# Decode attention over a key and value cache beside a small MLP: TensorE's program as loops, values always in one slot, part of w4 behind the last values

## The chip, the cores and the metric

The kernel runs on one core of a Trainium2 chip. The time is the device time of one execution in microseconds (us), the median of several. A profile of one execution is at hand beside it; its span runs from the first to the last instruction of the core.

## The reference

One token `x` (1024 values) goes through two branches and their sum is added to it.

```python
xn = _layernorm(x)
return x + _A_ref(xn, K, V, wq, wo) + _B_ref(xn, w1, w2, w3, w4)

# A: 32 query heads, 4 key/value heads, 65536 keys of 128 values each
q = (xn @ wq)                                # 1024 x 4096
p = softmax(q k^T * 128 ** -0.5)             # eight query heads share one K, V
A = (p @ v) @ wo                             # 4096 x 1024
# B: one position, so the shifted h is zero
hs = shift(gelu(layernorm(xn) @ w1)) @ w2    # 1024 x 1024 each
x1 = xn + hs
B = x1 + gelu(layernorm(x1) @ w3) @ w4       # 1024 x 3584, 3584 x 1024
```

All inputs are bf16. K and V are 67.1 MB each, the weights some 35.7 MB: 169.87 MB that are read once.

## The kernel before

**Slots and loads.** SBUF holds three slots of 32768 bf16 columns (8.39 MB over 128 partitions). K and V are cut into eight tiles (g, r): four heads g, two halves r of 32768 keys. `items` (L193 to L201) is the order of loads: wq, K(0,0), V(0,0), w3, K(0,1), V(0,1), wa (w1 and the first 14 rows of w4), then K and V in turn, wb (w4's last 14 rows and w2) ahead of the last V, and wo in five pieces. Item i goes to slot i mod 3 (L208), wo to the slot of the last K. All loads are issued by SyncE in program order (`load`, L211); each waits (L229) until what was computed from the slot's last content is done. The main loop (L566) computes item i and then issues the load of item i + 3.

**Order of work.** `Flow` is a small hand-written scheduler: it counts per engine, and each instruction waits on the counts of those that wrote or read its operands (L41). Engines run in the order of the program text.

**Products of one row.** q, w1's and w3's products (`rows_product`, L314 to L326) run unrolled, four column groups of TensorE at once. Weight rows of w2, w4 and wo (`rows_loop`, L328 to L341) run in TensorE loops (`Fori`): two or five rows per pass, two matmuls of 512 columns for each row, all adding up in `psR`. The last 22 rows of wo (`row_acc`, L534) run in four column groups.

**A K tile** (`compute_K`, L442): VectorE transposes the slot in four quarters `cg` (L449); after two quarters (after each, in the last tile) TensorE runs a loop of four passes over them, four or eight matmuls of 512 columns against `qst` (L455), into the four banks `sc`. Then the row maxima (L462), two small transposes on TensorE (L463, L468), the exponential on ScalarE (L471), and a transpose of the weights on VectorE (L473).

**A V tile** (`compute_V`, L495): 64 matmuls (L503) into `oacc`. The first half of a head is copied to `ob` (L509); after the second, `group_end` (L513) weights and adds both halves on VectorE, normalizes, and writes the columns `oT` that wo's rows are multiplied with.

**The end.** After the last `group_end` come wo's rows; the first ten rows' sum is folded into the output banks (L548, L549, L558), the last rows follow, and 2 KB go out (L561).

Of the kernel before, what the change touches and what calls it, by code (L numbers as in the profile page):

```python
# [16 lines left out]
WO_PIECES = (10, 10, 8, 3, 1)  # L17
WO_UNROLL = 5
CGS = 2


class Flow:


    def __init__(self, nc, ctx):
        self.nc = nc
        self.ctx = ctx
        self.engines = {"T": nc.tensor, "V": nc.vector, "S": nc.scalar, "G": nc.gpsimd, "Q": nc.sync}
        self.sems = {}
        self.counts = {}  # L30
        self.seen = {e: {} for e in self.engines}
        self.writer = {}
        self.readers = {}

    def sem(self, name):
        if name not in self.sems:
            self.sems[name] = self.ctx.enter_context(self.nc.semaphore(f"s_{name}"))
            self.counts[name] = 0
        return self.sems[name]

    def _wait(self, eng, reads, writes):  # L41
# [7 lines left out]
        for key in reads:  # L49
            if key in self.writer:  # L50
                token = self.writer[key]
                if token[0] != "T" or eng != "T":
                    add(token)
        for key in writes:
            if key in self.writer:
                token = self.writer[key]
                if token[0] != "T" or eng != "T":
                    add(token)
            for token in self.readers.get(key, ()):
                if token[0] != eng:  # L60
                    add(token)
        for name, value in need.items():
            if self.seen[eng].get(name, 0) < value:
                self.engines[eng].wait_ge(self.sem(name), value)
                self.seen[eng][name] = value
# [8 lines left out]
    def op(self, eng, reads, writes, emit, times=1):  # L74

        self._wait(eng, reads, writes)
        sem = self.sem(eng)

        def signal(ins):
            ins.then_inc(sem, 1)  # L80

        emit(signal)
        self.counts[eng] += times
        self._note((eng, self.counts[eng]), reads, writes)
# [8 lines left out]
    def one(self, eng, reads, writes, call):  # L93
        self.op(eng, reads, writes, lambda signal: signal(call(self.engines[eng])))
# [3 lines left out]
def kernel(  # L98
# [28 lines left out]
    assert S == 1 and DH == P and REP == 8 and HQ == 32 and DC == 8 and NOUT == 1024  # L127
# [4 lines left out]
    FW = F // 8  # L132
    assert FW <= 512 and F % 8 == 0 and FW % 16 == 0 and FW // 16 == FC and OC == 32
    NQ = NOUT // 4
    NH = NOUT // 2
    FH = FC // 2
# [9 lines left out]
    slots = [tile_sb([P, KEYS], BF16, f"slot{i}") for i in range(SLOTS)]  # L146
    work = tile_sb([P, HF * 512], BF16, "work")
    ob = tile_sb([P, 512], F32, "ob")
    xpad = tile_sb([P, DC, 32], BF16, "xpad")
    QS = P + 24  # L150
    qst = [tile_sb([P, 4, QS], BF16, f"qst{i}") for i in range(2)]
    qsel = tile_sb([P, 4, HQ], BF16, "qsel")
    ident_bf = tile_sb([P, P], BF16, "ident_bf")
    ident_f = tile_sb([P, P], F32, "ident_f")
    og = tile_sb([P, P + 1], F32, "og")
    msk = tile_sb([P, 4, 32], F32, "msk")
    hstrip = tile_sb([P, 192], BF16, "hstrip")
    gsel = tile_sb([P, P], BF16, "gsel")
    sel32 = tile_sb([P, 32], F32, "sel32")
    sel8 = tile_sb([P, 8], F32, "sel8")  # L160
    sel8x = tile_sb([P, 32], F32, "sel8x")
    mask16 = tile_sb([P, 16], F32, "mask16")
    mask64 = tile_sb([P, 64], F32, "mask64")
# [3 lines left out]
    lnb = tile_sb([P, 8, DC], F32, "lnb")  # L167
    x_bf = tile_sb([P, DC], BF16, "x_bf")
    xn2b = tile_sb([P, DC], BF16, "xn2b")
    qT = tile_sb([P, HQ], BF16, "qT")  # L170
    hf_f = tile_sb([P, FC], F32, "hf_f")
    hT = tile_sb([P, FC], BF16, "hT")
    gT = tile_sb([P, DC], BF16, "gT")
    o5 = tile_sb([P, 32], F32, "o5")
    oT = tile_sb([P, OC], BF16, "oT")
    rep = msk[0:1].rearrange("p a b -> p (a b)")

    sc = ps.tile([P, HF, 512], F32, name="sc")
    oacc = ps.tile([P, 512], F32, name="oacc")
    pm = ps.tile([P, 512], F32, name="pm")  # L180
    psR = ps.tile([P, 2, 512], F32, name="psR")
    psB = sc[:, 0, :]
# [7 lines left out]
    assert sum(WO_PIECES) == OC  # L190
    wo_start = [sum(WO_PIECES[:i]) for i in range(len(WO_PIECES))]

    items = [("wq",), ("K", 0, 0), ("V", 0, 0), ("w3",)]  # L193
    for g in range(HKV):
        for r in range(NT):
            if (g, r) != (0, 0):
                items += [("K", g, r), ("V", g, r)]
            if (g, r) == (0, 1):
                items += [("wa",)]
    items.insert(len(items) - 1, ("wb",))  # L200
    items += [("wo",)]  # L201
# [4 lines left out]
    one, op = fl.one, fl.op  # L206

    slot_of = [i % SLOTS for i in range(len(items))]  # L208
    slot_of[-1] = slot_of[items.index(("K", HKV - 1, NT - 1))]

    def load(i):  # L211
        item, s = items[i], slot_of[i]
        t, kind = slots[s], items[i][0]
# [4 lines left out]
        elif kind == "wa":  # L218
            loads = [(0, w1_v), (KEYS // 2, w4_v[:, 0:FH * NOUT])]
        elif kind == "wb":  # L220
            loads = [(0, w4_v[:, FH * NOUT:FC * NOUT]), (KEYS // 2, w2_v)]
# [3 lines left out]
        else:  # L225
            cache = A_k_cache if kind == "K" else A_v_cache
            _, g, r = item
            loads = [(0, cache[0, g, r * KEYS:(r + 1) * KEYS, :].rearrange("(p k) d -> p (k d)", p=P))]
        fl._wait("Q", [], [("slot", s), ("slot", s, 1)] + [("slot", s, q) for q in range(2, 5)] + [("kt", s, cg) for cg in range(4)])  # L229
        for n, (at, src) in enumerate(loads):  # L230
            key = ("slot", s) if n == 0 else ("slot", s, n)
            fl.dma("Q", f"slot{s}" if n == 0 else f"slot{s}_{n}", [], [key], t[:, at:at + src.shape[-1]], src)

    qrow = work[:, 0:1024].rearrange("p (b n) -> p b n", b=2)
    psel = work[:, 1024:1536].rearrange("p (b m) -> p b m", b=4)
    ones_f = og[:, 0:P]
    xr = work[:, 1536:2048]

    load(0)
    fl.dma("S", "x", [], ["x_bf"], x_bf[:], A_x[0, 0, :].rearrange("(p c) -> p c", c=DC))  # L240
    load(1)
    load(2)
    one("G", [], ["xr"], lambda e: e.memset(xr[0:33, :], 0.0))
    fl.dma("S", "x2", [], ["xr"], xr[0:33:32, :], A_x[0, 0, :].rearrange("(j n) -> j n", j=2))

    def ident(t, key):
        one("G", [], [key], lambda e: e.memset(t[:], 0.0))
        one("G", [key], [key], lambda e: e.affine_select(
            out=t[:], in_=t[:], compare_op=ALU.not_equal, fill=1.0, base=0, pattern=[[-1, P]],
            channel_multiplier=1))  # L250

    eps_t, negmean, rstd, ln_s1, ln_s2 = (sm[:, i:i + 1] for i in range(5))
    ident(ident_bf, "ident_bf")
    ident(ident_f, "ident_f")
    one("G", [], ["eps"], lambda e: e.memset(eps_t, LN_EPS))
    one("G", [], ["ones"], lambda e: e.memset(ones_f, 1.0))
    one("G", [], ["xpad"], lambda e: e.memset(xpad[:], 0.0))
    one("G", [], [("qst", 0)], lambda e: e.memset(qst[0][:], 0.0))
    one("G", [], [("qst", 1)], lambda e: e.memset(qst[1][:], 0.0))
    one("G", [], ["hstrip"], lambda e: e.memset(hstrip[:], 0.0))  # L260

    def v(reads, writes, call):
        one("V", reads, writes, call)

    v(["ident_f"], ["sel32"], lambda e: e.tensor_tensor(out=sel32[:], in0=ident_f[:, 0:32], in1=ident_f[:, 32:64], op=ALU.add))
    v(["ident_f", "sel32"], ["sel32"], lambda e: e.tensor_tensor(out=sel32[:], in0=sel32[:], in1=ident_f[:, 64:96], op=ALU.add))
    v(["ident_f", "sel32"], ["sel32"], lambda e: e.tensor_tensor(out=sel32[:], in0=sel32[:], in1=ident_f[:, 96:128], op=ALU.add))
    v(["sel32"], ["mask16"], lambda e: e.tensor_tensor(out=mask16[:], in0=sel32[:, 0:16], in1=sel32[:, 16:32], op=ALU.add))
    v(["ident_f"], ["mask64"], lambda e: e.tensor_tensor(out=mask64[:], in0=ident_f[:, 0:64], in1=ident_f[:, 64:128], op=ALU.add))
    v(["sel32"], ["dmask"], lambda e: e.reduce_sum(out=dmask[:], in_=sel32[:].rearrange("p (cg h) -> p cg h", h=8), axis=AX.X))  # L270
    v(["sel32"], ["mask4"], lambda e: e.reduce_sum(out=mask4[:], in_=sel32[:].rearrange("p (x dd) -> p dd x", dd=4), axis=AX.X))
    v(["sel32"], ["sel8"], lambda e: e.reduce_sum(out=sel8[:], in_=sel32[:].rearrange("p (cg h) -> p h cg", h=8), axis=AX.X))
    v(["sel8"], ["sel8x"], lambda e: e.tensor_copy(out=sel8x[:].rearrange("p (h dd) -> p h dd", dd=4),
                                                   in_=sel8[:].unsqueeze(2).to_broadcast([P, 8, 4])))
    iv = ident_bf[:].rearrange("p (b i r) -> p b r i", b=2, r=2)
    for b in range(2):
        for par in range(2):
            v(["ident_bf"], [("psel", b, par)], lambda e: e.tensor_copy(
                out=psel[:, 2 * b + par, :].rearrange("p (a i) -> p a i", a=4),
                in_=iv[:, b, par, :].unsqueeze(1).to_broadcast([P, 4, 32])))  # L280
    psel_keys = [("psel", b, par) for b in range(2) for par in range(2)]
    lead = ident_bf[:].rearrange("p (j u) -> p j u", u=32)[:, :, 0]
    v(["ident_bf", "hstrip"], ["hstrip"], lambda e: e.tensor_copy(
# [322 lines left out]
```

## Time and profile before

| | |
|---|---|
| median of 3 runs | 402.4 us (402.27 to 402.55) |
| the profiled execution | 402.23 us |
| its span | 400.1 us |
| TensorE, matmuls | 223.5 us busy, 1407 |
| VectorE | 210.5 us busy |
| ScalarE, GpSimd | 30.9 and 6.3 us busy |
| read from memory | 169.87 MB, 425 GB/s over the span |
| granted TensorE clock, mean | 0.803 |

The page has the busy time of each engine, the span in 40 slices of 10 us with a digit for the busy share in tenths, the load queues, and the chain of work that ended last, followed back from the last instruction. The chain in order of time is a view of its own: start, duration, what. "issue" in it is time for which no wait is seen. A row of the view of waits says which engine waited at which line for whom, the total, how often, and the longest.

### The profile page before, as it was taken

The numbers are of one execution on the slowest core, as the hardware profiler recorded it, in microseconds if no ns is written. First come the engines' busy times: TensorE is split into PE (matmuls) and PEld (weight loads), VectorE is DVE, ScalarE is ACT, GpSimd is POOL, SyncE is SP. The second block draws the span as 40 slices with busy tenths as digits, with TensorE's granted clock in tenths as the row PEclk, the third lists the DMA queues.
The fourth block names the chain that finished last, engine by engine and source line by source line (L and its number), as shares of the span: only waits on it lengthen the run. The fifth ranks groups of instructions, "written<-read, shape, count | busy, mean of one in ns | idle before, by whom it ended". The sixth has DMA issues, their size and how long they took to land.

```text
span 400.1 us, 4118 instructions
## 1 busy us (share of the span) xinstructions
PE 223.5 (56%) x1407; PEld 91.3 (23%) x1407; DVE 210.5 (53%) x191; ACT 30.9 (8%) x36; POOL 6.3 (2%) x28
## 2 busy tenths in 40 slices
PE   0263087360195563964395608845925194596985
PEld 0220033130042220421142203312402041232332
DVE  2201792210962448822972499269455963794421
ACT  1000000320001300003001000020020002000200
POOL 3000000000000000000000000000000000000000
PEclk9995579585589598795699567968988599799799
DMA  8999999999989999999999999999999999999995
GB/s 347 465 446 419 420 414 454 391 473 452 426 382 471 451 426 414 426 432 432 465 434 426 419 426 439 426 472 428 426 419 434 439 419 459 398 454 434 397 432 208
DMA packets 4054, 170.02 MB, mean 425 GB/s; under 512 B 582, under 2 KB 588, under 8 KB 844
## 3 DMA queue, kind: packets, MB, share of 16 engines
q1 hardware_dynamic: 3896, 169.87, 98.3%
q8 instruction: 8, 0.13, 0.1%
q10 hardware_dynamic: 148, 0.00, 0.0%
q14 instruction: 2, 0.02, 0.0%
HBM read 169.87 MB, written 0.00 MB: 425 GB/s over the span
## 4 chain that ended last, share of the span: by engine, by line
DMA 53%; PE 28%; DVE 13%; issue 4%; ACT 1%; SPq 1%; POOL 0%; ACTq 0%
DMA slot<-in_A_k_cache_dram 46%; PE sc L455 20%; DVE slot L449 10%; DMA slot<-in_A_wo_dram 7%; PE oacc L503 5%; PE psR L337 2%; DVE sm L462 2%; DVE work L473 1%; ACT work L471 1%; SPq L89 1%; PE sc L321 0%; DVE og L515 0%; ACT L471 0%; DVE sm L464 0%; PE pm L463 0%
## 5 line engine op out<-in xcount | busy, mean ns | idle before, releaser
L455 PE MATMUL sc<-slot,qst 128*128 x512 | 127.8, 407 | 77.4 <-DVE slot L449 76.4
L449 DVE STREAM_TRANSPOSE slot<-slot 128x4096 f32<-128x4096 f32 x32 | 139.4, 4413 | 29.7 <-DMA slot<-in_A_k_cache_dram 29.7
L455 PEld LDWEIGHTS sc<-slot,qst 128*128 128x128 bf16 x512 | 51.8, 101 | 154.2 <-issue 106.8
L503 PE MATMUL oacc<-slot,work 128*32 128x512 bf16 x512 | 45.7, 530 | 37.5 <-DVE work L473 21.9
L462 DVE TENSOR_REDUCE sm<-sc 128x1 f32<-128x2048 f32 x8 | 18.3, 2291 | 58.4 <-PE sc L455 58.4
L503 PEld LDWEIGHTS oacc<-slot,work 128*32 128x32 bf16 x512 | 19.0, 127 | 60.8 <-issue 56.9
L473 DVE STREAM_TRANSPOSE work<-work 128x2048 bf16<-128x2048 bf16 x8 | 18.5, 2312 | 21.2 <-ACT work L471 21.2
L471 ACT ACTIVATE work<-sc,sm 128x2048 bf16<-128x2048 f32 x8 | 15.7, 1967 | 147.1 <-DVE sm L469 147.1
L337 PE MATMUL psR<-slot,hT 128*1 x56 | 16.2, 438 | 0.5 <-issue 0.2
L515 DVE SCALAR_TENSOR_TENSOR og<-oacc,sm,og 128x128 f32<-128x128 f32 x16 | 5.6, 351 | 18.6 <-PE oacc L503 18.2
L321 PE MATMUL sc<-slot,xpad 128*32 128x512 bf16 (+1 forms) x144 | 11.1, 441 | 4.3 <-DMA slot<-in_A_wq_dram 4.3
L471 ACT ACT_TABLE_LOAD x3 | 3.8, 1283 | 117.5 <-DVE sm L469 117.5
L463 PE MATMUL pm<-ident_f,sm 128*1 128x128 f32 x8 | 2.2, 270 | 19.1 <-DVE sm L462 19.1
L294 PE MATMUL pm<-sm,og 128*128 128x1 f32 x4 | 1.2, 363 | 14.9 <-DVE sm L293 14.9
L337 PEld LDWEIGHTS psR<-slot,hT 128*1 x56 | 5.1, 92 | 10.9 <-issue 7.8
L321 PEld LDWEIGHTS sc<-slot,xpad 128*32 128x32 bf16 x144 | 5.4, 113 | 9.0 <-DMA slot<-in_A_wq_dram 4.4
L399 DVE TENSOR_TENSOR work<-pm,mask 128x448 f32<-128x448 f32 x1 | 0.6, 624 | 11.0 <-PE pm L394 11.0
L463 PEld LDWEIGHTS pm<-ident_f,sm 128*1 128x1 f32 x8 | 0.6, 79 | 23.0 <-DVE sm L462 23.0
L352 DVE CAST work<-sc 128x512 bf16<-128x512 f32 x1 | 0.7, 690 | 9.2 <-PE sc L321 9.2
L347 POOL COPY qst<-qsel 32x32 bf16<-32x32 bf16 x12 | 2.5, 206 | 189.0 <-PE sc L455 161.8
L337 PE MATMUL psR<-slot,oT 128*1 x20 | 4.5, 379 | 1.6 <-DVE oT L529 1.6
L509 ACT COPY ob<-oacc 128x512 f32<-128x512 f32 x4 | 2.3, 585 | 33.1 <-PE oacc L503 33.1
(99 smaller groups left out, 71.6 us busy)
## 6 DMA issues: line engine op xcount, KB each, us to landing
slot<-in_B_w_dram SPq DMA_DIRECT2D x1, 7168.0 KB, 50.8
slot<-in_B_w_dram SPq DMA_DIRECT2D x2, 3584.0 KB, 31.9
slot<-in_A_wo_dram SPq DMA_DIRECT2D x2, 2560.0 KB, 19.5
slot<-in_B_w_dram SPq DMA_DIRECT2D x2, 2048.0 KB, 30.1
slot<-in_A_wo_dram SPq DMA_DIRECT2D x1, 2048.0 KB, 26.7
slot<-in_A_wo_dram SPq DMA_DIRECT2D x1, 768.0 KB, 28.1
slot<-in_A_wo_dram SPq DMA_DIRECT2D x1, 256.0 KB, 28.4
slot<-in_A_k_cache_dram SPq DMA_DIRECT2D x8, 36.1
```

Source lines behind the costliest of these rows:

```text
L89: self.engines[eng].dma_start(out=out, in_=in_).then_inc(sem, 16)
L321: ins = nc.tensor.matmul(sc[32 * j:32 * j + 32, bk, 0:width], lhsT=xpad[:, c, :], rhs=wt[:, c, ch * width:(ch + 1) * width], start=(c == 0 ...
L337: ins = nc.tensor.matmul(psR[0:1, h, :], lhsT=lv[:, bass.ds(c, 1), u], rhs=wv[:, bass.ds(c, 1), u, h, :], start=False, stop=False, skip_gr ...
L347: lambda e: e.tensor_copy(out=qst[g % 2][sl, :, 24 + 32 * a:24 + 32 * a + 8], in_=qsel[sl, :, 8 * g:8 * g + 8]))
L449: v([("slot", s)], [("kt", s, cg)], lambda e: e.transpose(out=kf[:, cg, :], in_=kf[:, cg, :]))
L455: ins = nc.tensor.matmul(sc[:, bass.ds(hf, 1), :], lhsT=qst[g % 2][:, bp, 24 - 8 * cg:24 - 8 * cg + P], rhs=kr[:, cg, bass.ds(hf, 1), :, b ...
L462: v(["sc"], ["mx"], lambda e: e.reduce_max(out=mx, in_=sc[:].rearrange("p h n -> p (h n)"), axis=AX.X))
L463: one("T", ["mx", "ident_f"], ["pm"], lambda e: e.transpose(pm[0:1, 0:P], mx, ident_f[:]))
L471: one("S", ["sc", ("nball", r)], WORK + [("lall", r)], lambda e: e.activation(out=pT, in_=sc[:], func=ACTF.Exp, bias=nball[:, r:r + 1], sc ...
L473: v(["work"], ["work"], lambda e: e.transpose(out=pT, in_=pT))
L503: ins = nc.tensor.matmul(oacc[32 * u:32 * (u + 1), :], lhsT=pT[:, hf, 32 * t:32 * (t + 1)], rhs=vt[:, :, hf, t, :], start=(hf == 0 and t < 4),
L515: v(["oacc", ("wm", 1), "og"], ["og"], lambda e: e.scalar_tensor_tensor(out=og[:, 0:P], in0=oacc[:, P * cg:P * (cg + 1)], scalar=wm[:, 1, ...
```

## The change

It rewrites most of the kernel; the computation is the same.

- **Slots.** One tensor `home` holds the three slots side by side. wq goes to slot 1, w3 to slot 0, wa (w1, w2 and 13 rows of w4) to slot 2. After that K goes to slot 1 + r and V always to slot 0. The order of loads is wq, w3, wa, all K and V in turn, wb (w4's last 15 rows, in pieces of 9 and 6, to slot 1), wo in seven pieces. The last K comes in two pieces.
- **When loads are issued.** K(0,0) after wq's product, V(0,0) after w3's, K(0,1) after wa's rows; then, after the 64 value matmuls of each tile, the next V and the K after it. wo is issued after the last scores.
- **TensorE.** Its whole program is written once, as nested loops over heads, halves, quarters and passes, with addresses made of the loop counters. It does not wait on counts but takes tokens: it waits for a semaphore to reach 1 and takes 1 off. VectorE (VT), GpSimd (GT) and VectorE with ScalarE (RT) give them. The scores are accumulated onto zeros that ScalarE writes into `sc` after each tile.
- **Products of one row.** wq's and w3's products run in two passes of the same loop, one 512-column bank at a time, on one output row; 32 matmuls with one column turn the row into columns. The input's two layernorms run on one partition, on ScalarE and VectorE. w1's product is a loop as well. w2's and w4's rows come three to a pass.
- **The end.** 15 rows of w4 and 24 of wo run in one loop of 13 passes behind the last `group_end`, three rows to a pass, each pass taking a token that GpSimd gives when the piece has landed. Then the sum with the input's row is formed on VectorE, and the last eight rows of wo run in column groups as before.
- **One-pass loops.** TensorE's program, and that of the four other engines behind the first loads, each stand in a loop that runs once and whose closing branch carries a hint (`once`).

```diff
+@contextmanager
+def once(nc, engines, name):
+    regs = nc.alloc_registers(f"{name}_i", engines=engines)
+    nc.regs_mov(regs, 0)
+    nc.br(f"{name}_loop", engines=engines)
+    with nc.body(f"{name}_loop", valid_engines=engines):
+        marks = {e: nc.engines[e].mark_branch_hint_location() for e in engines}
+        yield
+        nc.regs_alu(regs, regs, 1, op=ALU.add)
+        for e, mark in marks.items():
+            nc.engines[e].br_lt(regs, 1, on_true=f"{name}_loop", on_false=f"{name}_end").branch_hint(mark)
+    nc.switch_bb(f"{name}_end")
...
-    items = [("wq",), ("K", 0, 0), ("V", 0, 0), ("w3",)]
...
+    items = [("wq",), ("w3",), ("wa",)]
     for g in range(HKV):
         for r in range(NT):
...
+            items += [("K", g, r), ("V", g, r)]
+    items += [("wb",), ("wo",)]
+    place = {"wq": 1, "w3": 0, "wa": 2, "V": 0, "wb": 1, "wo": 2}
+    slot_of = [1 + item[2] if item[0] == "K" else place[item[0]] for item in items]
...
+    def take(name, n=1):
+        te.wait_ge(tokens[name], n)
+        te.sem_inc(tokens[name], -n)
...
+        with te.Fori(0, 2) as i:
+            take("VT")
+            take("GT")
+            with te.Fori(0, 8) as ch:
+                for c in range(DC):
+                    ins = te.matmul(banks[0:1, bass.ds(ch, 1), :], lhsT=xn[:, bass.ds(i, 1), c],
+                                    rhs=home[:, bass.ds(i * (c * (F - NQ_ROW) - KEYS) + ch * 512 + KEYS + c * NQ_ROW, 512)],
+                                    start=(c == 0), stop=(c == DC - 1), skip_group_check=True)
+                ins.then_inc(sig, 1)
+            take("RT", 2)
+            with te.Fori(0, 8) as b:
+                for u in range(4):
+                    ins = te.matmul(pm[:, bass.ds(b * 4 + u, 1)], lhsT=row[:, bass.ds(b * 512 + u * P, P)],
+                                    rhs=ident_bf[0:1, 0:1], start=True, stop=True, skip_group_check=True)
+                ins.then_inc(sig, 1)
...
+        with te.Fori(0, HKV) as g:
+            with te.Fori(0, NT) as r:
+                with te.Fori(0, 4) as cg:
+                    take("VT")
+                    with te.Fori(0, HF) as hf:
+                        for bp in range(4):
+                            ins = te.matmul(sc[:, bass.ds(hf, 1), :],
+                                            lhsT=qst[:, bass.ds(g % 2, 1), bp, bass.ds(24 - cg * 8, P)],
+                                            rhs=kv[:, bass.ds(r * 16 + cg * 4 + hf + 16, 1), :, bp // 2, :, bp % 2],
+                                            start=False, stop=False, skip_group_check=True)
+                        ins.then_inc(sig, 1)
+                take("VT")
+                te.transpose(pm[0:1, 0:P], sm[:, 50:51], ident_f[:]).then_inc(sig, 1)
+                take("VT")
+                te.transpose(pm[:, P:P + 1], rep[0:1, :], ident_f[0:1, 0:1]).then_inc(sig, 1)
+                take("VT")
+                for y in range(64):
+                    u = y % 4
+                    ins = te.matmul(oacc[32 * u:32 * (u + 1), :], lhsT=work[:, 32 * y:32 * (y + 1)], rhs=vt[:, :, y, :],
+                                    start=(y < 4), stop=(y >= 60), tile_position=(0, 32 * u))
+                ins.then_inc(sig, 1)
+            take("VT")
+            te.matmul(pm[0:32, 0:P + 1], lhsT=sel8x[:], rhs=og, start=True, stop=True).then_inc(sig, 1)
...
+        for cg in range(4):
+            piece = cg // 2 if (g, r) == last_K[1:] else 0
+            v([], [("kt", ks, cg)], lambda e: e.transpose(out=kf[:, cg, :], in_=kf[:, cg, :]), tok="VT",
+              peek=[("slot", ks, piece), "sc", ("qst", g % 2)])
+            fl.pe([("kt", ks, cg), ("qst", g % 2)], ["sc"], HF)
...
+        fl.pe(["work", ("slot", vs, 0)], ["oacc"])
+        if not last:
+            s(["sm0"], ["sc"], lambda e: e.copy(out=sc, in_=zero.unsqueeze(2).to_broadcast([P, HF, 512])))
+            for n in (i + 3, i + 4):
+                if n < len(items) - 1:
+                    load(n)
...
+    for q, n in enumerate(W4_PIECES):
+        fl.token("G", [("slot", slot_of[-2], q)], "GT", n // UNROLL)
+        fl.pe(["cols", ("slot", slot_of[-2], q)], ["psR"], n // UNROLL)
...
+    for q, n in enumerate(WO_PIECES):
+        if wo_start[q] < WO_LOOP:
+            fl.token("G", ["oT", ("slot", so, q)], "GT", n // UNROLL)
+            fl.pe(["oT", ("slot", so, q)], ["psR"], n // UNROLL)
+    v(["psR", "work"], ["fold"], lambda e: e.tensor_tensor(out=fold, in0=psR[0:1].rearrange("o a n -> o (a n)"), in1=fold, op=ALU.add), tok="VT")
```

## The prediction

> **What bounds the kernel now.** I read the slices and queues of the page first, then the chain of waits, then single stages in the timeline.
>
> ```profile
> DMA  8999999999989999999999999999999999999995
> q1 hardware_dynamic: 3896, 169.87, 98.3%
> q8 instruction: 8, 0.13, 0.1%
> ```
>
> The one load queue is busy for 98.3% of the span: the kernel is bound by reading 169.87 MB once. Little can be won: 1.7% of 400.1 us is 6.8 us, and most of it lies ahead of the first byte and behind the last.
>
> ```profile
> 229.70 37.41 DMA slot<-in_A_k_cache_dram
> 305.89 38.49 DMA slot<-in_A_k_cache_dram
> 344.40 4.46 DVE slot L449
> 360.08 2.06 PE sc L455 x8
> 362.14 0.05 issue
> 362.19 1.04 PE sc L455 x4
> ...
> 368.24 28.37 DMA slot<-in_A_wo_dram
> ```
>
> Chain of waits (start, us, what). K tiles land at 267.11 and 344.38, four 8.39 MB loads apart: 77.27 / 4 = 19.31 us for one load, K+V of a tile 38.6. After the last K has landed, scores go on until 366.37; the end waits for wo (396.61), then 3.5 us of output.
>
> ```profile
> SPq L64 <- PE sc L455: 214.3, 8, 37.9
> SPq L64 <- PE oacc L503: 100.3, 7, 15.8
> ```
>
> SyncE's waits: loads are issued when scores (L455) or weighted sums (L503) have freed a slot. Three slots rotate, so V(t+1) is asked for when the scores of tile t end and K(t+2) when its PV ends. That keeps the queue full.
>
> **The change, part by part.** Bytes stay the same. What is new is the order: wq, w3, wa (w1, w2, 13 rows of w4) come first, V always goes to slot 0, K to slots 1 and 2 in turn. V(t+1) and, behind it on SyncE, K(t+2) are issued only when PV of tile t ends. At that moment the queue holds K(t+1) alone. Call L the time from a K's landing to its PV's end: the queue runs dry unless L plus the restart is under 38.6.
>
> *Restart.* The page's only dry start is wq: from issue to landing 22.1, of which 19.31 is transfer, so 2.8 at most; at least the issue's 0.4. I take 2.0.
>
> *A K tile.* DVE's four transposes take 4.41 each (L449). PE took 12.8 for three quarters of the last K (353.53 to 366.37), 4.28 each, in passes of four matmuls about 1.1 apart where the matmuls alone need 4 x 0.216: the sequencer sets this.
>
> ```profile
> 147.37 1.02 PE psR L337 x4
> 148.39 0.09 issue
> 148.48 1.02 PE psR L337 x4
> 149.51 0.02 issue
> 149.53 1.02 PE psR L337 x4
> ```
>
> The same in the weight rows: four matmuls with two moving addresses start every 1.07 (147.37 to 153.78, six passes). The new K loop has a third moving address (qst by g and by quarter) and an outer loop with a token wait, a token decrement, a counter and a taken branch. I add 0.5 per quarter: 4.8. Lower bound 4.41 (DVE sets the pace, all is hidden). Upper bound 6.6: 4 x 0.13 for four more addresses, 4 x 0.3 for index arithmetic repeated in each pass, 0.6 for the outer loop; nearest is the 4.28 row, so I stay low.
>
> *From scores to PV:* 292.09 to 300.35 is 8.26; with three tokens 8.4. *PV* took 6.58 at half clock (134.27) and 4.3 at full (378.2): I take 5.9, since PE waits 8.4 just before it and the clock row is at 0.5 then. A K stage that starts after an idle PE pays 1.2 for its first passes at half clock.
>
> So L is 4.41 + 0.35 + 19 + 1.2 + 8.4 + 5.9 = 39.3, more than 38.6 - 2.0. Behind the waiting V issue on SyncE stands the next K's issue, so both are late.
>
> *The head.* LayerNorm now runs on one partition: two copies and two squares of 1x1024 on ACT (some 1.05 each by L509's 0.585 for 512 columns), a table load of 1.28, small DVE steps; x lands at 13.4, so PE can start at about 24, wq having landed at 23.0. Products are no longer spread over four column groups (64 matmuls took 5.86, L321): 64 x 0.216 plus pass ends make 14.5, to 38.5, when K(0,0) is asked for. Copies 2.4; 32 single-column matmuls in 8 passes of 1.2 (the 1.07 row plus addresses; 1.07 to 1.33) make 9.6; 50.9 with the qT copy. w3's product 15.5 (cold), 66.4, V(0,0) asked for. Gelu: table 1.28 and 3584 columns at the exp's 1.97 per 2048, 4.8; second column loop 9.6; qsel 0.8; w1, 8 passes of two matmuls at 0.75, 6.0: 87.6. Rows of w2 and w4, 21 rows in 7 passes of 1.36: 97.1, K(0,1) asked for. Tile 0's transposes wait for the scores' zeroing behind w1's gelu (3.1): 90.7.
>
> The loads alone would have landed wa at 57.4, K(0,0) 76.7, V(0,0) 96.0, K(0,1) 115.3. K(0,1) is asked for at 97.1: the queue is dry for 3.1. PV of tile 0: PE from 97.1, +19.0, +8.4, +1.28 (exp table), +5.9 = 131.7, while K(0,1) landed at 118.4: dry for 15.3. This is the largest term, and nothing hides it: before, DVE and PE were as idle here, but the queue had work.
>
> *Tiles.* V lands at max(landing of the K before it, PV end + 2.0) + 19.31, the next K 19.31 later; transposes start when K has landed and DVE is free (3.4 behind PV where a group ends).
>
> ```
> tile  K lands  scores end  PV ends  queue dry after it
> 0      76.7     116.1      131.7    15.3
> 1     118.4     150.7      165.0     0
> 2     172.3     197.2      211.5     2.6
> 3     210.9     235.9      250.2     0
> 4     252.2     278.5      292.8     4.0
> 5     290.8     314.5      328.8     0
> 6     333.4     358.4      372.7     2.6
> 7     372.1     391.7      406.0
> ```
>
> *The tail.* V(3,1) lands at 394.0, w4's 15 rows at 403.0, wo at 422.4. PE is free at 408.2; 39 rows in 13 passes of 1.45 (six matmuls need 1.29, the 1.07 pass with two more matmuls 1.37, plus a token from GpSimd) end at 427.1, later than wo. The fold's sum of 1x1024 on DVE 1.4, its matmuls 0.6, the last rows 0.7: 429.8. Then 0.4 and 2.7 to the end as before: 433.0. The wait that took 28.37 for wo thus no longer ends last; the row loop does.
>
> *At nothing:* the one-pass loops (a move, an add, a branch per engine) lie behind the wait for x (DVE idle 8.24 there); without it some 0.3. Split K and more pieces of wo: issues of 0.4 each, with 28 us of transfers ahead of them.
>
> The sum is a span of 433.0 against 400.1; the profiled execution took 402.23 (median 402.4), 2.1 outside the span. **435.1.** Of the 33 added, 27.6 are dry queue, 7.1 the longer tail, less 1.9 that the landings as I add them are shorter than the trace's.
>
> [...]
>
> **Rivals.**
>
> *The queue stays full (other side).* If the head's small loops run at twice the speed I give them and the tile loop at DVE's pace, PV of tile 0 ends by 113 and the stream never dries. For it: all these durations are sequencer time that no row shows for these loops. Against it: 64 matmuls cannot take under 13.8, twice, and PE does them in order ahead of tile 0. It decides once tile 0's PV ends before K(0,1) lands. Then the code packets (q8, q14: 0.15 MB) mostly vanish, and the uneven end of the load engines (busy 0.83, 0.46, 0.03 in 394 to 397) narrows by about a microsecond: 401.
>
> *Loops cheap.* Quarter at 4.41: 425.2 by the same recurrence, 427.3 outside the span. With PV at 4.3, restart 1.1, products at 13.8 and no cold passes, 408.6: only tile 0's gap (7.8) is left. Middle 417.
>
> *Loops dear.* Quarter at 6.6: 479.5; middle 460. [...]
>
> *Only the tail.* Queue full but PE behind wo at the end: about 405; it is the low end of the cheap case.
>
> **Numbers.** Forecast (425 to 448) 0.46, cheap (403.2 to 425) 0.28, dear (448 to 482) 0.17, full queue 0.09, of which 0.06 faster and 0.03 the same. The bound of 0.2% is 0.8 us, about what a measurement of this kernel tells from no change. Faster 0.06, same 0.03, slower 0.91. The range 407 to 472 leaves out the full queue, a sliver of the cheap case (0.04) and the top of the dear one (0.05).
>
> **What would show it.** Right: the DMA row of the slices has digits under 9 near 120 us and every 77 us after; SyncE waits for the weighted sum just before dry stretches; in the chain PE takes a larger share than DMA, and the output waits for PE. Quarters of K: the pitch between token waits on PE near 4.8. Wrong: DMA at 9 throughout (the head is faster than I add up), or quarters at 4.4 with PE waiting for DVE (loop work hidden), or dry stretches of 10 and more in each tile (index work repeated).

## The result, and the profile after

The changed kernel takes 616.6 us (615.8 to 616.7) against 402.2 (401.9 to 402.55), a ratio of 1.533 (1.531 to 1.535): 214 us slower. 435.1 was forecast, with a range of 407 to 472. The direction was right, the added time wrong by a factor of six and a half (214 against 33). The page of the profile after, its first lines, slices, queues and two groups:

```profile
span 614.5 us, 5440 instructions
PE 318.1 (52%) x1422; PEld 109.0 (18%) x1422; DVE 209.0 (34%) x157; ACT 52.7 (9%) x51; POOL 7.4 (1%) x33
PEclk9997795977786767867777776867776877876799
DMA  9999939290059909960996399129936990683940
q1 hardware_dynamic: 4472, 169.87, 65.2%
q14 instruction: 2, 0.01, 0.0%
L328 PE MATMUL banks<-home,qst 128*128 x512 | 177.4, 506 | 166.1 <-PEq L270 152.2
L539 DVE STREAM_TRANSPOSE home<-home 128x4096 f32<-128x4096 f32 x32 | 142.0, 4439 | 180.9 <-PE banks L328 172.8
```

The load queue, busy for 98.3% before, is now busy for 65.2% with the same 169.87 MB: the DMA row falls to a digit from 0 to 3 in every tile. The last two lines say why. The same two groups in the kernel before:

```profile
L455 PE MATMUL sc<-slot,qst 128*128 x512 | 127.8, 407 | 77.4 <-DVE slot L449 76.4
L449 DVE STREAM_TRANSPOSE slot<-slot 128x4096 f32<-128x4096 f32 x32 | 139.4, 4413 | 29.7 <-DMA slot<-in_A_k_cache_dram 29.7
```

VectorE's 32 transposes of K cost what they cost before (4439 ns each against 4413), but VectorE sat idle for 180.9 us ahead of them (29.7 before, all of it for loads), and 172.8 of it ended with TensorE's scores (L328). TensorE sat idle for 166.1 us ahead of those scores, 152.2 of it until its sequencer had passed the token wait (L270). Each of the two waits for the other. VectorE's and TensorE's timelines in tile 2 (start, duration, what, and in brackets the idle time before and who ended it):

```profile
233.62 4.42 DVE L539 STREAM_TRANSPOSE home<-home 128x4096 f32<-128x4096 f32 x1
245.00 4.45 DVE L539 STREAM_TRANSPOSE home<-home 128x4096 f32<-128x4096 f32 x1 [6.96 <-PE banks L328]
256.36 4.45 DVE L539 STREAM_TRANSPOSE home<-home 128x4096 f32<-128x4096 f32 x1 [6.92 <-PE banks L328]
```

```profile
239.10 4.62 PE L328 MATMUL banks<-home,qst 128*128 x12 [6.37 <-PEq L270]
243.92 1.04 PE L328 MATMUL banks<-home,qst 128*128 x4 [0.20 <-issue]
250.43 4.27 PE L328 MATMUL banks<-home,qst 128*128 x12 [5.47 <-PEq L270]
255.28 1.04 PE L328 MATMUL banks<-home,qst 128*128 x4 [0.58 <-issue]
```

A quarter comes every 11.4 us: 4.45 of transpose, then 6.9 in which TensorE takes the token and runs the four passes over it (1.0 and 5.9). The forecast had 4.8. The loads show what follows. SyncE's waits:

```profile
SPq L65 <- PE banks L340: 403.2, 7, 62.9
SPq L65 <- PE banks L280: 83.6, 2, 47.5
```

For 403.2 us in seven waits (100.3 before) SyncE stood behind PV (the 64 value matmuls of a tile, L340) with the next V and K. K tiles land some 58 us apart (five steps from 217.2 to 506.8), where the loads alone need 38.6; from K(1,0)'s landing at 217.2 to the end of its PV at 292.8 pass 75.6, where the forecast's L is 39.3. For 16.4 of the 75.6 K waits until VectorE has finished the tile before (233.62).

### The profile page after: what moved, and what is told of

It is laid out like the page before. It is cut to its first block, busy times and chain, and to the rows that moved or that the text cites. A ratio compares the mean times of both kernels' runs of the same rounds, so it can differ in the third digit from the quotient of the medians.

```text
span 614.5 us, 5440 instructions
## 1 busy us (share of the span) xinstructions
PE 318.1 (52%) x1422; PEld 109.0 (18%) x1422; DVE 209.0 (34%) x157; ACT 52.7 (9%) x51; POOL 7.4 (1%) x33
## 3 DMA queue, kind: packets, MB, share of 16 engines
q1 hardware_dynamic: 4472, 169.87, 65.2%
HBM read 169.87 MB, written 0.00 MB: 276 GB/s over the span
## 5 line engine op out<-in xcount | busy, mean ns | idle before, releaser
L328 PE MATMUL banks<-home,qst 128*128 x512 | 177.4, 506 | 166.1 <-PEq L270 152.2
L539 DVE STREAM_TRANSPOSE home<-home 128x4096 f32<-128x4096 f32 x32 | 142.0, 4439 | 180.9 <-PE banks L328 172.8
L328 PEld LDWEIGHTS banks<-home,qst 128*128 x512 | 58.2, 114 | 284.7 <-issue 265.1
L340 PE MATMUL banks<-home,scratch 128*32 128x512 bf16 x512 | 44.9, 527 | 40.0 <-PEq L270 40.0
L280 PE MATMUL banks<-home,xn 128*1 x128 | 43.7, 419 | 20.1 <-PEq L270 15.9
L553 ACT ACTIVATE scratch<-banks,sm 128x2048 bf16<-128x2048 f32 x8 | 15.7, 1967 | 349.8 <-DVE sm L552 349.8
L545 DVE TENSOR_REDUCE sm<-banks 128x1 f32<-128x2048 f32 x8 | 18.3, 2291 | 56.0 <-PE banks L328 56.0
L340 PEld LDWEIGHTS banks<-home,scratch 128*32 128x32 bf16 x512 | 18.9, 127 | 62.8 <-issue 59.0
L312 PE MATMUL banks<-home,cols 128*1 x120 | 28.5, 378 | 2.6 <-issue 1.7
L555 DVE STREAM_TRANSPOSE scratch<-scratch 128x2048 bf16<-128x2048 bf16 x8 | 18.5, 2311 | 18.8 <-ACT scratch L553 18.8
## 6 DMA issues: line engine op xcount, KB each, us to landing
home<-in_A_wo_dram SPq DMA_DIRECT2D x4, 1536.0 KB, 11.4
```

Source lines behind the costliest of these rows:

```text
L280: ins = te.matmul(banks[0:1, bass.ds(ch, 1), :], lhsT=xn[:, bass.ds(i, 1), c], rhs=home[:, bass.ds(i * (c * (F - NQ_ROW) - KEYS) + ch * 51 ...
L312: ins = te.matmul(psR[0:1, h, :], lhsT=lv[:, bass.ds(c, 1), u], rhs=wv[:, bass.ds(c, 1), u, h, :], start=False, stop=False, skip_group_che ...
L328: ins = te.matmul(sc[:, bass.ds(hf, 1), :], lhsT=qst[:, bass.ds(g % 2, 1), bp, bass.ds(24 - cg * 8, P)], rhs=kv[:, bass.ds(r * 16 + cg * 4 ...
L340: ins = te.matmul(oacc[32 * u:32 * (u + 1), :], lhsT=work[:, 32 * y:32 * (y + 1)], rhs=vt[:, :, y, :], start=(y < 4), stop=(y >= 60), tile ...
L539: v([], [("kt", ks, cg)], lambda e: e.transpose(out=kf[:, cg, :], in_=kf[:, cg, :]), tok="VT", peek=[("slot", ks, piece), "sc", ("qst", g ...
L545: v(["sc"], ["mx"], lambda e: e.reduce_max(out=mx, in_=sc.rearrange("p h n -> p (h n)"), axis=AX.X), tok="VT")
```

## The experiments

Each is one run beside one of the kernel before, except where an interval or a range of several runs is given.

**The wait taken away.** `peek` adds its names to those that the transpose waits for, and the scores' `fl.pe` two lines below writes `sc`. For quarter 0 the last writer of `sc` is ScalarE's zeroing; for the quarters after, it is TensorE's scores of the quarter before.

```diff
-              peek=[("slot", ks, piece), "sc", ("qst", g % 2)])
+              peek=[("slot", ks, piece), ("qst", g % 2)] + (["sc"] if cg == 0 else []))
```

> Of the changed kernel this run takes away one wait: the transposes of K quarters 1, 2 and 3 no longer wait for the scores of the quarter before (quarter 0 still waits for the zeroing). Theory A (that wait makes VectorE and TensorE take turns, 11.4 us a quarter, and the turns are the main loss): the quarter falls to the four passes of about 1.62 that TensorE's sequencer needs, 6.5 us; by the recurrence of the prediction with the durations that the changed kernel's trace shows (products 24.0 each, rows 1.61, quarter 6.5) the time is 494, between 485 and 510. Rival B (one home for V keeps the queue dry whatever the quarters do): the time stays above 590, and the landings stay some 58 us a tile apart. Rival C (TensorE's passes alone are the quarter): VectorE's transposes come one behind the other at 4.45 but the quarters of TensorE still stand 11 apart, 600 or more.

509.2, 107.4 less. The 24 waits were worth 4.47 each, the length of one transpose, which now lies beside TensorE's work. VectorE's group, and TensorE's timeline of one quarter and the start of the next:

```profile
L539 DVE STREAM_TRANSPOSE home<-home 128x4096 f32<-128x4096 f32 x32 | 139.2, 4406 | 8.2 <-ACT banks L492 8.1
```

```profile
218.82 1.05 PE L328 MATMUL banks<-home,qst 128*128 x4 [1.15 <-PEq L270]
220.42 1.04 PE L328 MATMUL banks<-home,qst 128*128 x4 [0.56 <-issue]
222.05 1.04 PE L328 MATMUL banks<-home,qst 128*128 x4 [0.58 <-issue]
223.67 1.05 PE L328 MATMUL banks<-home,qst 128*128 x4 [0.58 <-issue]
225.86 1.04 PE L328 MATMUL banks<-home,qst 128*128 x4 [1.14 <-PEq L270]
```

Of VectorE's 180.9 us of idle time 8.2 are left. But the quarter is 7.04 (218.82 to 225.86), not 6.5 and far from 4.8: passes 1.61 apart, and another 0.6 for the loop around them. Theory A holds, near the upper end of its range; B and C fall. The passes take this long at full clock too: the granted clock is 1.0 from 218.8 to 232.9, and the four passes over a quarter take 5.9 there as in the changed kernel, where the clock is at 0.5 for part of most of them.

**Scores written out.** In addition TensorE's loops over halves, quarters and passes become program text, and the loop over heads one over pairs of heads, so that no address of the scores is made from a counter.

```diff
-        with te.Fori(0, HKV) as g:
-            with te.Fori(0, NT) as r:
-                with te.Fori(0, 4) as cg:
+        def group(g):
+            for r in range(NT):
+                for cg in range(4):
...
-                    with te.Fori(0, HF) as hf:
+                    for hf in range(HF):
...
+        with te.Fori(0, HKV // 2) as gg:
+            group(0)
+            group(1)
```

> As the run with the wait taken away, and TensorE's loops over quarters, passes and tiles of a group are written out (the loop over pairs of groups is left), so that no matmul of the scores has an address in a register. Theory A: the second loss is index work repeated in each pass (1.62 us for four matmuls); written out, a quarter goes at VectorE's pace or at the 1.1 of the kernel before, 4.4 to 4.6, and the time is 445 to 449, some 45 under the run with the wait alone. Rival E (the matmuls themselves, at half clock, take the 1.62): the quarter stays near 6 and the time within 10 of the run with the wait alone. Rival F (written out, the code of two groups is fetched from memory again): instruction packets come back in q8 or q14 and TensorE's sequencer stands in places for a microsecond or more.

448.1, another 61.1 less. The view of one line of the run with the wait alone taken away shows what went, at L328 on TensorE's sequencer (how many, shortest, median and longest ns, first and last start):

```profile
L328 PEldq FUSED_REGOPS  x768: 42/74/124, 119.2 to 460.7; - x192
```

Six such instructions of index arithmetic for every four matmuls, repeated in each pass, and a taken branch of 0.22. The branch alone does not make the difference: a pass of the kernel before has it too (0.215 at 356.21), with four such instructions of 42 to 46 ns, and takes 1.1. Without both TensorE needs 3.65 for a quarter at full clock, and VectorE waits for loads, as two lines of this run's page show:

```profile
q8 instruction: 5, 0.08, 0.1%
L543 DVE STREAM_TRANSPOSE home<-home 128x4096 f32<-128x4096 f32 x32 | 139.5, 4414 | 38.2 <-DMA home<-in_A_k_cache_dram 30.1
```

Rival E falls. Instruction packets are back (q8), as rival F said, but the time is theory A's, and no stall goes with them: every stand of TensorE's sequencer of a microsecond or more in the tiles ends at a token wait, the one behind the loop's closing branch (267.4 to 274.2) with VectorE's first quarter of the tile (269.7 to 274.1).

**K asked for earlier.**

```diff
         last = t == len(tiles) - 1
+        if i + 4 < len(items) - 2:
+            load(i + 4)
...
             for n in (i + 3, i + 4):
-                if n < len(items) - 1:
+                if n < len(items) - 1 and not (n == i + 4 and n < len(items) - 2):
```

> As the run with the wait taken away, and K(t+2) is asked for right behind the scores of tile t, ahead of V(t+1), instead of behind PV of tile t. Theory A with the dry queue as third loss: TensorE's own work of a tile (4 x 6.5 + 8.4 + 5.9 = 40.3) sets the pitch instead of 43.8, so some 25 under the run with the wait alone, about 470. Rival G (the dry queue costs nothing beside the passes): within 8 of the run with the wait alone.

507.8: the run with the wait alone less 1.4. Rival G holds. K now lands long before it is needed, and the tiles still come 45 apart, because TensorE's quarters and VectorE's group end set the pace. My 40.3 left out that VectorE begins a tile's transposes only behind `group_end`: they begin 40.7 apart within a head (205.26, 245.99) and 50.5 where a head ends between them (245.99, 296.44).

**The head.**

```diff
-        with te.Fori(0, 2) as i:
+        for i in range(2):
...
-            with te.Fori(0, 8) as ch:
+            for ch in range(8):
```

> The run with scores written out, and in the head the two products are written out too (their 64 matmuls have fixed addresses) and x's column load is asked for before wq and before x's row. Theory A (index work repeated per matmul stretches a product from some 14.5 to 24.0): each product falls to 14 to 17, PE starts at 24 instead of 27, and K(0,0), V(0,0) and K(0,1) are asked for some 12, 21 and 21 earlier; by the recurrence 427 to 432, some 18 under the 448 of the run before. Rival (cold clock: the products' matmuls at half clock take the time): products stay above 20 and the time above 440.

428.6, 19.5 less (430.7, 430.0 to 431.4, in three more runs below). x's columns are also asked for first, ahead of wq and x's row. The products took 23.9 each in the changed kernel (27.14 to 51.09, 63.76 to 87.68) and take 15.5 here (25.78 to 41.33, 53.28 to 68.73). The line of the product in the changed kernel's trace:

```profile
L280 PEldq FUSED_REGOPS  x240: 37/69/147, 27.0 to 87.2; - x120
```

Per matmul it is a pair of 142 and 37 ns, 0.31 with the gaps, and TensorE waits for it. The rival with the cold clock falls. x's columns land at 11.1 instead of 25.4; in the changed kernel they were the second small load on ScalarE's queue and came in behind wq.

**All four together.**

> The run before with K(t+2) asked for right behind the scores of tile t. With quarters at VectorE's pace the loads bound the tiles, so here the order of the issues should show: the steady dry stretches go, 4 to 6 less than the run before (about 423). If V's one home costs nothing in this state: within 1.5 of the run before. Compared with the kernel before, what is left is the head's dry queue and the row loop of the tail.

427.0, 1.6 less: between the two expectations. It is one run against one, and the kernel without this step gave 428.6 to 431.4 in four, so the 1.6 is not told from nothing. K comes early, and the stretch in which the queue is dry moves to the last V (K(3,1) lands at 336.8, V(3,1) at 385.9 instead of 387.1).

**The wait put into the kernel before.**

```diff
-        n_cg = 1 if (g, r) == (HKV - 1, NT - 1) else CGS
+        n_cg = 1
...
-                v([("slot", s)], [("kt", s, cg)], lambda e: e.transpose(
+                v([("slot", s)] + (["sc"] if cg else []), [("kt", s, cg)], lambda e: e.transpose(
```

> The kernel before with the wait alone: the transposes of K quarters 1, 2 and 3 wait for the scores of the quarter before (and scores are done quarter by quarter in every tile, not two quarters at a time). Theory A: transpose 4.45, release 0.35 and scores 4.28 come one behind the other, 9.1 a quarter; a tile's pitch is then 4 x 9.1 + 8.4 = 44.7, some 3.4 more where a group ends, against 38.6 of loads: 445 to 475, about 455. Rival (in this kernel VectorE has slack behind the loads, and the turns are hidden): 402 to 410.

507.0, 104.9 more than the kernel before, with none of the new loops. The edit also has the scores done quarter by quarter in every tile; in the last tile of the kernel before, where that is so already, a tile's scores take 17.2 (349.20 to 366.37) against 15.8 to 16.4 in four of the others, so it is a small part. The mechanism is theory A's, and the cost is larger than the 43 to 73 that I expected. The groups of scores and transposes:

```profile
L455 PE MATMUL sc<-slot,qst 128*128 x512 | 167.1, 494 | 148.9 <-DVE slot L449 148.8
L449 DVE STREAM_TRANSPOSE slot<-slot 128x4096 f32<-128x4096 f32 x32 | 142.1, 4441 | 149.6 <-PE sc L455 138.2 <-DMA slot<-in_A_k_cache_dram 11.4
```

A matmul of the scores takes 494 ns in the mean, 407 in the kernel before: behind an idle stretch TensorE is at half clock for 3.1 to 5.0 us of a quarter (the granted clock is 0.50 in 245 to 251, where a quarter starts at 247.28), and for none of the four quarters that have no such stretch ahead of them. So the scores of a quarter mostly take 5.3 (4.1 to 4.4 in the last tile of the kernel before, which runs the same loop without a pause), and quarters are mostly 10.2 apart. VectorE's idle time ends with TensorE's scores, as in the changed kernel.

**V asked for behind PV, in the kernel before.** Three versions. The first two missed their aim: in one (the first part of the diff) SyncE's wait was for PV of two tiles earlier, in the other (the second part) the order of its program changed but nothing made it wait.

```diff
+        if kind == "V" and "oacc" in fl.writer:
+            fl._wait("Q", ["oacc"], [])
...
-        if i + SLOTS < len(items) and i + SLOTS < len(items) - 1:
-            load(i + SLOTS)
+        for n in ([held.pop()] if held and it[0] == "V" else []) + [i + SLOTS]:
+            if n < len(items) - 1:
+                if items[n][0] == "V" and it[0] == "K":
+                    held.append(n)
+                else:
+                    load(n)
```

> The kernel before, where only the load of each V waits until PV of the tile before has ended, as with one home for V; the order of the loads and the slots stay. The forecast's mechanism (the queue runs dry when PV ends later than the next K has landed): in the trace of the kernel before, PV ends 38.7 to 43.3 behind its K's landing and the pitch of the loads is 38.6, so with a restart of 2.0 the queue is dry for 2 to 6 in each tile from tile 2 on: 412 to 430, about 418. Rival (hidden, the tiles catch up): 402 to 405.

> In the run before this one, V's load waited for PV of two tiles earlier (PV of the tile before was not yet written down when the load was), so it did not put the forecast's mechanism to the test; 402.3 says only that that wait is free. Here, from the load of V(1,1) on, the kernel before issues each V right behind PV of the tile before, and the next K behind it, as the changed kernel does. The forecast's mechanism: PV ends 38.7 to 43 behind its K's landing against a pitch of 38.6, with a restart of 2.0, so the queue is dry for 2 to 6 in each of five tiles: 408 to 422, about 414. Rival (hidden): 402 to 405.

402.3 (one run) and 402.4 (ratio 1.0002, 0.9992 to 1.0013): no effect, and no test of the forecast's mechanism. The third has both, the order and the wait:

> The order of the run before and the wait itself: SyncE issues each V, from V(1,1) on, only when PV of the tile before has ended (in the run with the order alone SyncE's program stood that way, but nothing made it wait, and V was still issued at 178.0, before PV ended at 192.8). The forecast's mechanism: in that trace PV ends at 192.8, 230.0 and 271.5 where the next K has landed at 190.3, 228.9 and 267.5; with a restart of 2.0 the queue is dry for 4.5, 3.1 and 6.0 there, and for less once the tiles have shifted: 408 to 420, about 412. Rival (hidden, PV comes earlier once it need not wait for a busy VectorE): 402 to 404.

414.2 (412.9 and 415.6; ratio 1.030, 1.015 to 1.044). SyncE issues V(1,1) at 192.3, K(1,1) had landed at 189.8, and V(1,1) lands at 215.6, 25.8 behind it instead of 19.3. V(2,1) and V(3,0) land 21.9 and 21.8 behind their K. The three together are 11.6 of the 13.4 by which the span of this run is longer. Its DMA row:

```profile
DMA  9999999999999999994999999979998999999994
```

So the forecast's dry queue is real, at 12 us in a kernel whose L is 39 to 43 (two runs, and an interval that reaches from 1.5% to 4.4%). With the wait away, the scores written out and the head mended L is 35 to 36 (K(1,0) lands at 172.3, its PV ends at 208.0), and behind V(0,1) no load of K or V is late by more than 1.4.

**The one-pass loops.** First the changed kernel without them, then the kernel before with them, with and without the hint.

```diff
-    with once(nc, OrderedEngineSet([E.PE]), "tensor"):
-        tensor_program()
+    tensor_program()
...
-    rest.enter_context(once(nc, OrderedEngineSet([E.DVE, E.Activation, E.Pool, E.SP]), "rest"))
```

> The changed kernel without the loops of one pass and their branch hints (nothing else is changed; TensorE's inner loops stay). Theory A: those loops cost a move, an add and a branch per engine behind the wait for x, so 616.6 within 1.5. Rival D (the hints or the branch back make the engines fetch their program anew in each tile): 6 us or more away from 616.6, and the number of instruction packets changes.

> The kernel before with every engine's program inside a loop of one pass with a branch hint, as in the changed kernel, and nothing else. In the forecast this cost nothing (some 0.3 at most). Theory H (an engine that falls through the branch at the end must first fetch what stands behind it): VectorE's last drain comes some 2.8 late, as in the changed kernel (614.1 against 611.3 of the other engines), and the time is 404.5 to 405.5. Rival: no change, 401.8 to 402.6.

> As the run before, with the loop of one pass but without the branch hint. If the hint makes the engines fetch the loop's head in place of what follows: no late drain, 401.8 to 402.8. If the loop itself (its own block at the end) does it: the same as with the hint, 404.5 to 405.5.

610.9, 5.7 less, between the two bounds that were set; but 402.55 (1.001, 1.0000 to 1.0019) and 402.28 (0.9999, 0.999 to 1.0009) in the kernel before. Theory H's late drain is in the changed kernel only: VectorE's last at 614.1, those of the others at 611.3 to 611.5. Hence three versions on one chip, on the kernel with wait, scores and head mended:

```diff
-            nc.engines[e].br_lt(regs, 1, on_true=f"{name}_loop", on_false=f"{name}_end").branch_hint(mark)
+            nc.engines[e].br_lt(regs, 1, on_true=f"{name}_loop", on_false=f"{name}_end")
```

> The kernel with wait, scores and head undone (428.6 in one look), timed again as the basis of the two runs that follow: 427.5 to 429.5, with VectorE's last instructions some 2.5 behind the other engines'.

> The same with the loops of one pass and without their branch hints. Theory H1 (the hint makes VectorE fetch the loop's head in place of what stands behind it): no late VectorE at the end, 2 to 3 less than the run before. Theory H2 (the block behind the loop's end makes it late whatever the hint): as the run before within 0.8.

> The same without the loops of one pass. H1 and H2: no late VectorE at the end, 2 to 3 less than the first of these three (425.6 to 426.6). Rival H3 (what is late is the place of VectorE's code, not the loop): the late end stays, within 0.8 of the first. If it is more than 4 less, the loops also cost in the head, as the 5.7 of the changed kernel without loops suggest.

430.7 (430.0 to 431.4) with loop and hint, 427.9 (427.3 to 428.8) with the loop alone, 429.0 (427.1 to 432.4) without. With the hint VectorE's last instruction comes at 429.64, that of the others at 427.3; in the two other profiles it comes with them (425.89, 425.02). The hint costs 2.8 by the medians, 2.3 of it in this late end. The third is too scattered to tell whether the loop itself costs anything here; in the kernel before it does not. The reads of instructions (q14) fit H1's reason: without the hint (the loop alone) two of 8 KB come in the middle, at 161.8 and 359.6, and none at the end; with it the one read comes at 427.85, while VectorE stands. In the kernel before the hint takes away the second read too (381.0), and nothing there comes late. Why not, and what the other 3 of the 5.7 were (1.7 are there when K(0,1) is asked for, at 117.3 instead of 119.0), stays open.

## Why the prediction was wrong, step by step

**The step that failed is the K tile:** "I add 0.5 per quarter: 4.8 ... upper bound 6.6", and L = 4.41 + 0.35 + 19 + ... It takes VectorE's four transposes as running ahead of TensorE, one behind the other. I had read `sc` among the names the transpose waits for, and costed it for tile 0 as the zeroing; that the scores of quarter 0 become its next writer, and that quarters 1 to 3 therefore wait for TensorE, I did not follow. The quarter was 11.4. Taking this one wait away returned 107.4 of the 214; the same wait put into the kernel before cost 104.9.

**The same step, its size.** Unhindered, the quarter is 7.04, above my upper bound. I had listed index work repeated in each pass (4 x 0.3) as the unlikely end and chose the low one because the 4.28 row was nearest. That row has two addresses from one counter; these are made of up to three counters. The parts of that bound (0.13, 0.3 and 0.6) were estimates, for which I named no row. A pass is 1.61, not 1.1, and the loop around the four takes another 0.6: writing the scores out, with the wait already away, returned 61.1.

**The head.** Products 14.5 and 15.5 forecast, 23.9 measured, for the same reason; written out, 15.5 both. PE's start 24 forecast, 27.1 measured, since x came at 25.4 and not at 13.4. Column loops (9.6 forecast, 8.5 measured), w1 (6.0, 6.1) and the seven row passes (9.5, 9.6) were right. K(0,1) was asked for at 119.0 instead of 97.1; the run with the head mended got 19.5 back.

**What is left comes near the forecast's 33, in part by luck.** With wait, scores and head mended, the run of 428.6 has a span of 426.9, 26.8 over the kernel before. (Undone in this order, the wait, the scores and the head gave back 107.4, 61.1 and 19.5 of the 214; in another order the parts could differ.) The last of wo lands at 416.5 instead of 396.6, 19.9 later, 16.0 of it dry queue in tile 0 (5.5 before K(0,1), 10.5 before V(0,1); 18.4 forecast). The 9.2 forecast for the later tiles are not there (at most 3.9), because L is 35 to 36 and not 39.3 once the quarters go at VectorE's pace. A load asked for with the queue dry took 21.8 (V(1,0) in the changed kernel, 230.73 to 252.56), so the restart is 2.5; I took 2.0. From the landing of wo to the end it is 4.4 longer, because the row loop ends behind wo (13 passes of 1.6, 1.45 forecast; 7.1 forecast in all). The last 2.4 are VectorE's late end under the hint, which I had at nothing; that 4.4 and 2.4 come near the 7.1 is luck. The DMA row of that run has its gap in the head only:

```profile
DMA  9999999996927999999999999999999989998980
```

**The signs.** "Dry stretches of 10 and more in each tile" I had named as the sign of repeated index work. They came, but half of the time lost was the wait: a sign that two causes share does not tell them apart; the pitch of the quarters on both engines does. The rival *loops dear* had the index work right and too small (quarter 6.6, 7.04 measured without the wait), and knew nothing of the wait. No read of instructions shows in the tiles: the changed kernel's page has no q8 row, and no instruction packet at all comes between 100 and 600. In the run with the wait taken away the taken branch that closes a half takes 0.22 (251.20), and the next token wait stands 0.6 behind it (251.82).

No version beat the kernel before.

## What to carry to other kernels

For each new wait, write down who was the last to write or read what it names at that iteration, not at the first: a name that guards an initial state turns into a handshake as soon as the other engine writes it in the same loop. Two engines that took turns cost the sum of their times (4.45 and 6.9, 11.4 a quarter) instead of the larger (7.04 with the wait taken away), and behind the idle time TensorE came back at a lower clock as well (0.50 granted in 245 to 251 in the kernel before with the wait, and mostly 5.3 for the scores of a quarter instead of 4.1 to 4.4). An address made of several loop counters was paid for at each matmul here; before a program is rolled up, count its index instructions per pass against the matmuls beside them.

## What the runs showed of the hardware that was not expected

- TensorE's sequencer took a pair of register instructions of 142 and 37 ns for each matmul with an address of two counters, 0.31 in all, and a product of 64 such matmuls took 23.9; with fixed addresses, in the run with the head mended, it took 15.5, 0.24 a matmul.
- A load of 2 KB issued 0.6 us behind a 2 KB load on ScalarE's queue, with wq issued at 0.96 on SyncE's, landed at 25.4, behind all of wq; issued ahead of both it landed at 11.1.
- Scores of one quarter, in the same loop of four passes, took 4.1 to 4.4 without a pause ahead of them (the last tile of the kernel before) and, in that kernel with the wait, mostly 5.3 after 4.8 us of idle time, 3.4 of it at a granted clock of 0.5.
- The branch hint on a loop that runs once made VectorE's last instruction 2.3 to 2.8 us late in the changed kernel and its versions, and not in the kernel before.
